# Seven products for eight: Strassen's scheme for the upper half of a gated block, with its sums on VectorE

## Chip, cores, metric

One core of a Trainium2 chip. The metric is the device time of one launch in microseconds (us), slowest core, median of several executions.

## The reference

```python
# attention: 4 batches, 8 heads, 768 positions, head size 64; a position attends to those
# whose six hash bits (signs of q @ proj) equal its own
mask = q_bucket[:, :, :, None] == k_bucket[:, :, None, :]
scores = np.where(mask, scale * np.matmul(q, k.transpose(0, 1, 3, 2)), -1e9)
attn = softmax(scores)                      # float32
x = (attn @ v)  ->  (3072 tokens, 512)
# gated block: w_gate, w_val (512, 1536), w_out (1536, 512)
g = x @ w_gate
silu = g * (1.0 / (1.0 + np.exp(-g)))
val = x @ w_val
return (silu * val @ w_out).astype(np.float32)
```

`x @ w_gate` and `x @ w_val` are the upper products, the product with `w_out` is the down product. The tokens of one batch are 768, in two halves of 384.

## The kernel before

The gated block of one batch is cut into 72 pieces ("atoms") that are woven into the attention of the next batch, in the order in which they are emitted. Each engine works off its own instructions in that order. After the last batch's attention, only the gated block is left.

```python
def norm(u):                                   # ends one half of a head pair
    ps = side_bank("sum")                      # a bank of its own
    for h in range(2):
        nc.tensor.matmul(ps[...], ones, t[:, h, :], start=True, stop=True)
    nc.vector.reciprocal(r, ps[:, 0:HQ])
    ...
    nc.vector.scalar_tensor_tensor(out=xT[b][:, pr, half * HQ : (half + 1) * HQ], ...)
    if pr == NP - 1 and half == 1:
        push_ffn(b)                            # x of the batch is complete: queue its atoms
...
def up(f, half, w, name):                      # 48 of these a batch: four fp32 matmuls each
    ps = bank(name)
    for j in range(NJ):
        nc.tensor.matmul(ps[:, 0:HQ], w[:, j, f * P : (f + 1) * P],
                         x[:, j, half * HQ : (half + 1) * HQ], start=j == 0, stop=j == NJ - 1)
    ...                                        # g: tanh on ScalarE, gate on VectorE; val: VectorE
def down(half, i, fs):                         # 24 of these a batch: three fp32 matmuls each
    for f in fs:
        nc.tensor.matmul(ps, hs[half][f][:, i * P : (i + 1) * P], wo[:, f, :], ...)
...
def hash_blocks():                             # hash of the next head pair
    ps = front_bank("hps")
    where = [(name, half) for name in "kq" for half in range(2)]
    for i, (name, half) in enumerate(where):
        nc.tensor.matmul(ps[i * BLOCK : (i + 1) * BLOCK, 0:HQ], hash_w[name][:, 0:BLOCK], ...)
    for i, (name, half) in enumerate(where):
        for to in (0, D):
            sign(name, half, ...)              # k: VectorE (kb), q: ScalarE (qb)
...
for u in range(0, N + 2, 2):                   # one iteration: two units of attention
    score(u); score(u + 1)                     # exp on ScalarE
    while due:
        norm(due.pop(0))
    for x in left:
        attend(x)                              # av on TensorE, acc on VectorE
    ...
    credit += rate                             # 3.1
    while atoms and credit >= 1.0:
        credit -= 1.0
        atoms.pop(0)()
        ...
```

The softmax here doesn't subtract the row's maximum and nothing guards it: scores larger than these inputs give would overflow.

## Time and profile before

| | before |
|---|---|
| time, median of 3 | 1139.44 us (1139.39 to 1139.5) |
| span of the profiled run | 1137.4 us |
| TensorE, VectorE, ScalarE busy | 1126.2, 538.4, 269.1 us |
| TensorE without work | 11.2 us (span less busy) |
| mean granted TensorE clock | 1.000 |

TensorE works 99% of the span. Of the 11 us without work, some 9 lie at the start and at the end, where the last output is written. Time can only be won where TensorE has less to do. The lines for this are in the prediction.

### The profile page before, as it was taken

What the parts mean: (1) busy time and instruction counts of PE and PEld (TensorE: products, weight loads), DVE (VectorE), ACT (ScalarE), POOL (GpSimd) and SP (SyncE); (2) the same over time, 40 slices, a digit from 0 to 9 for tenths busy, and PEclk for the clock granted to TensorE, in tenths of its full rate; (3) what the DMA queues carried; (4) which work ended last, traced back from release to release, by engine and by line L of the source; (5) the groups of instructions that cost most, each with busy time, mean ns of one, the idle gap of its engine ahead of it and who ended that gap; (6) DMA issues with size and microseconds to landing.
All of it is one profiled execution on the core that took longest, in us unless ns stands there. A gap on an engine that the chain in (4) does not pass through costs nothing.

```text
span 1137.4 us, 10768 instructions
## 1 busy us (share of the span) xinstructions
PE 1126.2 (99%) x4357; PEld 548.9 (48%) x4357; DVE 538.4 (47%) x783; ACT 269.1 (24%) x413; POOL 21.0 (2%) x57
## 2 busy tenths in 40 slices
PE   8999999999999999999999999999999999999998
PEld 3444445555444455555544445555544445555543
DVE  4899989899942244344442244444342222222100
ACT  4545221212212222122221223222131121010000
POOL 1000000000000000000000000000000000000000
PEclk9999999999999999999999999999999999999999
DMA  5333422423200220010002021010000000000000
GB/s 140 90 95 67 110 74 88 103 87 103 75 33 19 46 43 1 15 28 14 1 15 46 19 61 29 14 28 1 15 0 10 19 19 9 1 1 0 1 28 28
DMA packets 97842, 44.74 MB, mean 39 GB/s; under 512 B 86016, under 2 KB 90112, under 8 KB 97792
## 3 DMA queue, kind: packets, MB, share of 16 engines
q1 hardware_dynamic: 92032, 26.03, 10.0%
q0 software_dynamic: 4960, 17.83, 5.0%
q8 instruction: 34, 0.56, 0.2%
q10 hardware_dynamic: 800, 0.20, 0.1%
q14 instruction: 16, 0.13, 0.0%
HBM read 37.75 MB, written 6.29 MB: 39 GB/s over the span
## 4 chain that ended last, share of the span: by engine, by line
PE 96%; DVE 3%; ACT 0%; DMA 0%; issue 0%; SPq 0%; DVEq 0%; ACTq 0%
PE po L399 22%; PE g L378 22%; PE val L378 22%; PE sc L325 13%; PE av L336 11%; PE sum L357 2%; PE hps L276 2%; DVE acc L344 1%; PE tps L258 1%; PE hps L285 1%; DVE r L360 0%; DMA kraw<-in_k_dram 0%; PE idle L134 0%; DVE kb L271 0%; DVE wv L226 0%
## 5 line engine op out<-in xcount | busy, mean ns | idle before, releaser
L378 PE MATMUL val<-xT,wv 128*128 128x384 f32 x768 | 266.5, 490 | 0.3 <-DVE wv L226 0.3
L378 PE MATMUL g<-xT,wg 128*128 128x384 f32 x768 | 266.2, 490 | 0.0
L399 PE MATMUL po<-wo,ht 128*128 128x512 f32 x576 | 254.6, 597 | 0.0
L327 ACT ACTIVATE A<-sc 128x768 f32<-128x768 f32 x192 | 154.8, 812 | 192.6 <-PE sc L325 170.9
L378 PEld LDWEIGHTS val<-xT,wv 128*128 128x128 f32 x768 | 143.7, 190 | 111.5 <-issue 7.3
L378 PEld LDWEIGHTS g<-xT,wg 128*128 128x128 f32 x768 | 143.7, 190 | 110.8 <-DVE acc L344 6.0
L399 PEld LDWEIGHTS po<-wo,ht 128*128 128x128 f32 x576 | 107.4, 190 | 140.3 <-issue 138.9
L360 DVE RECIPROCAL r<-sum 128x384 f32<-128x384 f32 x32 | 81.8, 2556 | 176.1 <-PE sum L357 176.1
L325 PE MATMUL sc<-qT,kT 64*128 64x384 f32 x768 | 155.1, 482 | 0.0
L336 PE MATMUL av<-A,vraw 128*64 128x386 f32 x768 | 144.1, 496 | 0.0
L385 DVE SCALAR_TENSOR_TENSOR t<-t,g 128x384 f32<-128x384 f32 x96 | 53.0, 552 | 188.5 <-ACT t L384 188.5
L384 ACT ACTIVATE t<-g 128x384 f32<-128x384 f32 x96 | 47.1, 491 | 398.5 <-PE g L378 393.6
L344 DVE TENSOR_TENSOR acc<-acc,A 128x768 f32<-128x768 f32 x128 | 122.2, 955 | 34.0 <-ACT A L327 29.0
L390 DVE SCALAR_TENSOR_TENSOR ht<-t,val 128x384 f32<-128x384 f32 x96 | 52.9, 551 | 101.5 <-PE val L378 101.1
L336 PEld LDWEIGHTS av<-A,vraw 128*64 128x64 f32 x768 | 49.4, 136 | 81.3 <-issue 79.0
L325 PEld LDWEIGHTS sc<-qT,kT 64*128 64x128 f32 x768 | 68.7, 189 | 21.4 <-issue 21.4
L325 PE MATMUL sc<-qb,kb 64*128 64x384 bf16 x384 | 63.6, 328 | 0.8 <-DVE kb L271 0.8
L325 PEld LDWEIGHTS <-kb 64*128 64x128 bf16 x384 | 18.6, 93 | 68.7 <-issue 54.3
L403 ACT COPY o<-po 128x512 f32<-128x512 f32 x24 | 14.1, 586 | 155.6 <-PE po L399 155.3
L269 ACT ACTIVATE qb<-hps,columns 32x384 bf16<-32x384 f32 (+1 forms) x48 | 27.7, 577 | 77.3 <-DVE kb L271 44.6
L271 DVE TENSOR_SCALAR kb<-hps,columns 32x384 bf16<-32x384 f32 (+1 forms) x48 | 32.1, 669 | 24.2 <-PE hps L285 17.2
L340 DVE SCALAR_TENSOR_TENSOR acc<-A 128x768 f32<-128x768 f32 x32 | 30.4, 951 | 0.0
(69 smaller groups left out, 350.8 us busy)
## 6 DMA issues: line engine op xcount, KB each, us to landing
vraw<-in_v_dram SPq DMA_DIRECT2D x16, 384.0 KB, 3.1
words<-in_moe_w_val_dram POOLq DMA_DIRECT2D x12, 512.0 KB, 3.7
words<-in_moe_w_out_dram POOLq DMA_DIRECT2D x12, 512.0 KB, 3.5
out_dram<-o SPq DMA_DIRECT2D x24, 256.0 KB, 2.0
words<-in_moe_w_gate_dram POOLq DMA_DIRECT2D x10, 512.0 KB, 3.8
qraw<-in_q_dram SPq DMA_DIRECT2D x48, 96.0 KB, 3.1
kraw<-in_k_dram SPq DMA_DIRECT2D x46, 96.0 KB, 3.0
qraw<-in_q_dram SPq DMA_DIRECT2D x8, 192.0 KB, 3.5
```

The source lines that it names most:

```text
L271: nc.vector.tensor_scalar(o, ps[at, 0:HQ], scalar1=above_k[to], scalar2=times_k[to], op0=ALU.is_gt, op1=ALU.mult)
L325: nc.tensor.matmul(sc[:, h, 0:HQ], x["k", n][rows, ks], x["q", n][rows, qs], start=start, stop=not start)
L327: nc.scalar.activation(ring[u % RING][:, :, 0:HQ], sc[:, :, 0:HQ], AF.Exp, scale=SCALE)
L336: nc.tensor.matmul(ps[h * D : (h + 1) * D, 0:AW], raws["v", n][:, h, c, :], a[:, h, :], start=c == 0, stop=c == NCH - 1)
L340: nc.vector.scalar_tensor_tensor(out=acc[n, half], in0=ring[(u - 1) % RING][:, :, 0:HQ], scalar=S * EPS / P, in1=a[:, :, 0:HQ], op0=ALU.ad ...
L344: nc.vector.tensor_tensor(acc[n, half], acc[n, half], a[:, :, 0:HQ], op=ALU.add)
L360: nc.vector.reciprocal(r, ps[:, 0:HQ])
L378: nc.tensor.matmul(ps[:, 0:HQ], w[:, j, f * P : (f + 1) * P], x[:, j, half * HQ : (half + 1) * HQ], start=j == 0, stop=j == NJ - 1)
L384: nc.scalar.activation(t, ps[:, 0:HQ], AF.Tanh, scale=0.5)
L385: nc.vector.scalar_tensor_tensor(out=t, in0=t, scalar=1.0, in1=ps[:, 0:HQ], op0=ALU.add, op1=ALU.mult)
L390: nc.vector.scalar_tensor_tensor(out=ht, in0=now["t"], scalar=0.5, in1=ps[:, 0:HQ], op0=ALU.mult, op1=ALU.mult)
L399: nc.tensor.matmul(ps, hs[half][f][:, i * P : (i + 1) * P], wo[:, f, :], start=f == 0, stop=f == NF - 1)
```

## The change

Two 128-column blocks of a weight and the two token halves form a 2 by 2 block product over the two halves of the inner dimension 512. It takes eight block products, or seven by Strassen's scheme (in Winograd's form) with sums before and after. A block product is two fp32 matmuls of 128x384, half of what an `up` atom does. In each of batches two to four, twelve groups (six pairs of blocks, two weights) of seven products replace 48 atoms. The first batch keeps the plain products, as VectorE is still at work on the weights then.

Other parts of it: the bank kept for the norm's sums and the hash goes, these use score tiles (two, of two banks each), and the products get three banks for two. x is kept in one tile per head pair, some buffers shrink to make room, and the credit counts a product as 1 and every other atom as 2. Cut to its core:

```diff
-    aux_ps = ctx.enter_context(tc.tile_pool(name="aux_ps", bufs=1, space=PSUM))
-    mm_ps = ctx.enter_context(tc.tile_pool(name="mm_ps", bufs=2, space=PSUM))
+    mm_ps = ctx.enter_context(tc.tile_pool(name="mm_ps", bufs=3, space=PSUM))
...
-        ps = side_bank("sum")
+        ps = score_tile("sum")[:, 0, :] if atoms else bank("sum")
...
+    def up_strassen(x, hs, first):
+        lo, hi = halves
+        ...                                    # eight sums of x, emitted at once, on VectorE:
+            (t3[:, j], x[2 + j][:, hi], x[j][:, hi], subtract),
+            (t2[:, j], t3[:, j], x[j][:, lo], add),
+            (x[j][:, hi], x[j][:, hi], x[j][:, lo], subtract),
+            (t4[:, j], t2[:, j], x[2 + j][:, lo], subtract),
+        def combine(i):                        # sums of weights
+            if first:
+                nc.vector.tensor_tensor(s3, a11, s3, op=ALU.subtract)
+            nc.vector.tensor_tensor(s2, a22, s3, op=ALU.subtract)
+            nc.vector.tensor_tensor(s1, s2, a11, op=ALU.add)
+            nc.vector.tensor_tensor(s4, a12, s2, op=ALU.subtract)
+        ...
+            def step(n):                       # one atom: one product
+                if n == 0:
+                    combine(i + 1)
+                if n in (0, 1, 2, 6):
+                    now[n % 6 if n < 6 else 6] = bank("up")[:, 0:HQ]
+                if n == 0:
+                    product(b(0), a11, [x[j][:, lo] for j in range(2)], True)
+                    nc.scalar.copy(now["p1"], b(0))
+                elif n == 1:
+                    product(b(1), s2, [t2[:, j] for j in range(2)], True)
+                    add(now["u2"], now["p1"], b(1))
+                elif n == 2:
+                    product(b(2), s1, [x[j][:, hi] for j in range(2)], True)
+                    add(now["y"], now["p1"], b(2))
+                elif n == 3:
+                    product(b(0), a12, [x[2 + j][:, lo] for j in range(2)], False)
+                    done(0, 0, b(0), tile_of())   # gate: tanh on ScalarE, then VectorE
+                elif n == 4:
+                    product(b(1), s3, [t3[:, j] for j in range(2)], False)
+                    ...
+        combine(0)
+        for i in range(len(groups)):
+            group(i)
...
-        credit += rate
-        while atoms and credit >= 1.0:
+        credit += 6.2 if n < 2 * NP else 5.6
+        while atoms and credit >= atoms[0][0]:
```

## The prediction

> **What bounds the kernel now.** I read the page's busy shares first, then the slices, the chain and the groups, and last the timeline around the points where a batch of the gated block begins.
>
> ```profile
> PE 1126.2 (99%) x4357; PEld 548.9 (48%) x4357; DVE 538.4 (47%) x783; ACT 269.1 (24%) x413; POOL 21.0 (2%) x57
> PE   8999999999999999999999999999999999999998
> DVE  4899989899942244344442244444342222222100
> PEclk9999999999999999999999999999999999999999
> PE 96%; DVE 3%; ACT 0%; DMA 0%; issue 0%; SPq 0%; DVEq 0%; ACTq 0%
> L378 PE MATMUL val<-xT,wv 128*128 128x384 f32 x768 | 266.5, 490 | 0.3 <-DVE wv L226 0.3
> L378 PE MATMUL g<-xT,wg 128*128 128x384 f32 x768 | 266.2, 490 | 0.0
> L360 DVE RECIPROCAL r<-sum 128x384 f32<-128x384 f32 x32 | 81.8, 2556 | 176.1 <-PE sum L357 176.1
> L385 DVE SCALAR_TENSOR_TENSOR t<-t,g 128x384 f32<-128x384 f32 x96 | 53.0, 552 | 188.5 <-ACT t L384 188.5
> L344 DVE TENSOR_TENSOR acc<-acc,A 128x768 f32<-128x768 f32 x128 | 122.2, 955 | 34.0 <-ACT A L327 29.0
> ```
>
> TensorE is busy in every slice, at full clock, and 96% of the chain is its own. So time taken out of it counts in full as long as nothing makes it wait. The kernel calls 192 upper matmuls a batch; 1536 records for four batches means two records per fp32 call. The mean of 490 ns counts overlapped records twice, so I take the spacing from the last stage, where nothing else is interleaved. There a block of 8 records takes 2.58 us, 0.3225 us a record:
>
> ```profile
> 952.97 2.58 PE g L378 x8
> 955.55 2.58 PE val L378 x8
> ```
>
> The other thing to read is where a batch begins (here batch three, inside attention), and what the hash does to the queues:
>
> ```profile
> 673.94 0.34 PE L325 MATMUL sc<-qb,kb 64*128 64x384 bf16 x2
> ...
> 674.97 1.62 ACT L327 ACTIVATE A<-sc 128x768 f32<-128x768 f32 x2 [0.44 <-PE sc L325]
> 675.66 0.87 PE L357 MATMUL sum<-acc,ones 128*64 128x384 f32 x4
> 676.35 1.47 PE L336 MATMUL av<-A,vraw 128*64 128x386 f32 x8
> 676.57 2.56 DVE L360 RECIPROCAL r<-sum 128x384 f32<-128x384 f32 x1 [10.37 <-PE sum L357]
> 677.75 2.85 PE L378 MATMUL g<-xT,wg 128*128 128x384 f32 x8
> 679.19 0.62 DVE L363 SCALAR_TENSOR_TENSOR xT<-avs,e,r 128x384 f32<-128x384 f32 x1
> ...
> 761.47 2.72 DVE L271 TENSOR_SCALAR kb<-hps,columns 32x384 bf16<-32x384 f32 x4 [0.26 <-PE hps L285]
> 764.28 2.33 ACT L269 ACTIVATE qb<-hps,columns 32x384 bf16<-32x384 f32 x4 [6.97 <-DVE kb L271]
> 766.64 0.49 ACT L384 ACTIVATE t<-g 128x384 f32<-128x384 f32 x1
> ```
>
> TensorE starts the gated block at 677.75, although the last half of x is normed only at 679.8: the first blocks take the other half. Nothing waits today. The last three lines show the hash: VectorE reads its bank, then ScalarE, and the tanh behind it waits.
>
> **What the Trainium skill says.** (1) "TensorE: Matmul & The Clock Gate", Back-to-back issue gap: N/2.4 + 2.5 ns, 162.5 ns at N = 384. The trace's 322.5 ns a record is about twice that, as if each record passed its columns twice; I use the trace's number. (2) "VectorE: DVE Perf Modes", The TRN2 errata: an fp32 tensor_tensor takes (N+151)/0.96 ns. For 768 that is 957 ns, the trace has 955, so they agree. As estimates, 384 columns take 557 ns (the trace's 552 for a scalar_tensor_tensor from PSUM fits) and 256 take 424 ns. (3) "PSUM — Partial Sum Buffer", PSUM bank collisions: two engines must not be in the same bank and quadrant at once, reads included. The trace agrees: qb begins 0.09 us after kb ends. (4) The TensorE page again, What's actually happening: after an idle window of some 3.4 us the clock falls to half, until a busy window has passed. The kernel before has no such gap, and its clock line is flat.
>
> **The change, part by part.**
>
> *Removed.* Two blocks of outputs by two weights halves need 8 products before and 7 after. Per batch 192 calls become 168 (12 groups of 7 products of 2 calls): 48 records fewer, x 0.3225 = 15.5 us. Three batches: **46.4 us**, all on the path. A perfect result would be 1093.
>
> *Added on VectorE.* Per group: three weight sums of 256 (1.27 us) and six sums of 384 with a PSUM operand (3.34 us); the four gatings (2.21 us) were there. That is 6.82 us a group beside 14 x 0.645 = 9.03 us of TensorE. Per batch also eight sums of x (4.5 us), and in batch two a fourth weight sum a group (5.1 us in all). Sum: 12 x (1.27 + 3.34) + 4.5 = 59.8 us a batch, 185 us in all. VectorE goes to about 725 us, two thirds of the span. ScalarE gains 36 copies of 0.48, 17 us. On average both fit, so the question is bursts.
>
> *Steady work.* In the last stage I followed banks by hand: a product bank is wanted again two products (2.58 us) after its last matmul, and the two or three VectorE operations that free it (plus tanh of 0.49) take 1.0 to 1.4 us. It holds; no stall. In the interleaved iterations TensorE has 1.72 (scores) + 1.45 (av) + 5.6 products x 1.29 = 10.4 us; VectorE has 1.9 (acc) + 5.6 x 0.97 = 7.4, more with a norm (3.3), two transposes (1.9) or the hash (2.7).
>
> *Start of each changed batch.* This is the largest loss. The x sums need the half that the last norm writes, and the code queues on VectorE: reciprocal, xT (3.3 us together), eight x sums, then the weight sums, and only product one (t2, s2) can then go. Counted from the iteration's start: TensorE does scores, sums, av and product zero until 5.35 us. VectorE starts the reciprocal at 2.65 and has xT at 5.95. Operations without a wait between them follow each other some 0.08 us faster than their durations (in the trace the transpose starts 0.47 us after a 0.55 us gating), so eight sums at 0.48 and s2 end at 10.2, 10.6 with the extra sum of batch two. Stall: 5.25 and 4.85 us. In the last batch no av products lie in between: the norm's sums end, product zero takes 1.3 us, VectorE needs 2.6 + 0.7 + 3.8 + 0.4 = 7.6: stall 6.3. Together **16.4 us**.
>
> *Hash.* The hash now uses a score tile, and the copy of product zero queues on ScalarE behind qb, which waits for kb, which waits for VectorE's backlog. Following the queues by hand: in the second iteration of a batch, product three, which adds to the bank that this copy reads, waits about 2.75 us; one pair later the second score waits about 1 us for the hash's tile; one more pair later 0.2; in the down products about 0.7. That is some 4.7 us a batch, **9.5 us** for the two interleaved ones.
>
> *Norm sums.* They now take the score tile whose exp ends at 675.8 in the lines above, where the sums began at 675.66: 0.2 us each, 24 norms: **5 us** for the three interleaved stages.
>
> *Clock.* Three start stalls of 5 to 6 us are long enough to lose the clock; a window of 3.4 us at half speed costs 1.7 us, some 1 us on average each, as it isn't certain: **3 us**.
>
> Sum: 46.4 - 16.4 - 9.5 - 5 - 3 = 12.5 us gained. **1127 us**, 1.1% faster.
>
> **Rivals.**
>
> A: *the count of products alone*. Bursts are absorbed by the third bank and by the scores, where VectorE catches up. For it: VectorE stays at two thirds, and TensorE stands idle for 11 us at most today. Only a few starts would be lost: 1098 to 1108. Against it: the start's order of work is in the code, and VectorE runs in order.
>
> B: *VectorE becomes the bound inside attention*. An iteration with norm and transposes has 7.4 + 3.3 - 1.0 + 1.9 = 11.6 us of VectorE beside 10.4 to 11.1 of TensorE; gate groups add about 1 us of waiting on tanh. If every such iteration loses 2 us and every hash 3, another 10 to 15 us go and the time is 1138 to 1143. Against it: a pair of six iterations has about 56 us of VectorE in 66 of TensorE, and the remaining iterations pay it back.
>
> C: *each product of four records costs more than half a block of eight*, because more waits stand before a weight load; the first block after a switch takes 2.78 for 2.58. With 0.1 us on 252 products that would be 25 us, and the gain would be gone: about 1150. Against it: in the last stage blocks that each wait for a bank follow at an even 2.58.
>
> **Range and chances.** The saving is sure to a microsecond or two; the losses are an estimate of 34 us from following queues by hand, and could be 15 (rival A in part) or 50 (B in part). This gives 1104 to 1143. Over 2% faster means under 1116.7, losses below 24 us: 0.3. Slower by 2% needs losses of 69 us: 0.05. Within 2%: 0.65.
>
> **What would show it.** Upper product records should fall by 144, at an unchanged spacing (1.29 us a product). At each of the three batch starts TensorE should stand still for 5 to 6 us before a product, waiting on a VectorE weight sum or x sum, and the clock line may dip there. Sums should wait on the exp; a product or a score should wait near each hash. VectorE should show near 725 us busy. The prediction is wrong if those starts have no gap, if the spacing of products in the last stage is above 1.35 us, or if TensorE's idle time is spread over all interleaved products instead of these places.

## The result, and the profile after

1129.97 us (1128.81 to 1130.28, four runs) against 1139.47 of the kernel before in the same rounds. The ratio is 0.9914, interval 0.9897 to 0.9931. Ratios here are the mean time of one kernel's fast runs over that of the other's fast runs of the same rounds, so not quite the ratio of the medians quoted.

The parts of the page that answer to those shown of before (busy time, slices, chain):

```profile
PE 1093.0 (97%) x4213; PEld 525.5 (47%) x4213; DVE 700.7 (62%) x1143; ACT 284.8 (25%) x449; POOL 21.1 (2%) x57
...
PE   8999999999999989999999997999999997999998
...
DVE  4899989999932267777761337667674223667400
...
PEclk9999999999999989999999998999999998999999
...
PE 89%; DVE 6%; ACT 3%; issue 1%; DMA 0%; POOL 0%; SPq 0%; ACTq 0%; DVEq 0%; POOLq 0%
```

TensorE has 144 records fewer (4357 to 4213), as the count of products says. VectorE rose from 538 to 701 us. TensorE's line and its clock line now have dips in the same three slices, and VectorE and ScalarE have come into the chain. Who TensorE waited for, longest first (total us, times, longest), in the view of waits:

```profile
PE up L450 <- DVE ws L442: 15.8, 3, 6.0
PE up L450 <- ACT ht L483: 2.9, 1, 2.9
PE up L450 <- DVE c L378: 2.3, 1, 2.3
PE sum L359 <- ACT A L329: 2.2, 8, 1.0
...
PE sc L327 <- ACT qb L271: 0.9, 2, 0.6
```

Line 450 is the product, 442 the weight sum s2, 483 the copy of product zero, 378 the gate, 359 the norm's sums, 329 the exp, 271 the sign of q's hash. Three waits, one per changed batch, make up 15.8 us. Here is the last batch's, in the timeline (start, us, engine, line; the releaser in brackets):

```profile
944.84 0.87 PE L359 MATMUL sum<-acc,ones 128*64 128x384 f32 x4
...
945.64 1.56 PE L450 MATMUL up<-xT,wg 128*128 128x384 f32 x4
945.75 2.56 DVE L362 RECIPROCAL r<-sum 128x384 f32<-128x384 f32 x1 [14.85 <-PE sum L359]
...
948.37 0.62 DVE L365 SCALAR_TENSOR_TENSOR xT<-avs,e,r 128x384 f32<-128x384 f32 x1
948.91 1.02 DVE L423 TENSOR_TENSOR xc<-xT 128x384 f32<-128x384 f32 x2
...
951.72 1.02 DVE L423 TENSOR_TENSOR xc<-xc,xT 128x384 f32<-128x384 f32 x2
952.66 0.41 DVE L442 TENSOR_TENSOR ws<-wg 128x256 f32<-128x256 f32 x1
...
953.22 2.90 PE L450 MATMUL up<-xc,ws 128*128 128x384 f32 x4 [6.02 <-DVE ws L442]
...
955.91 2.05 PE L450 MATMUL up<-xT,ws 128*128 128x384 f32 x4
957.80 1.45 PE L450 MATMUL up<-xT,wg 128*128 128x384 f32 x4
```

Product zero goes at 945.64. VectorE then works without a pause through the reciprocal, xT, eight sums of x and one weight sum, and product one can go 6.02 us late. It is also slow: the next product starts 2.69 us after it, the one after 1.89 us later, and only then comes the usual 1.29 (957.80 to 959.09). The wait has cost the clock: the profile shows it at half from 950.28 to 957.10.

**Where the 46.4 us went**, by the trace. TensorE without work rose from 11.2 to 35.2 us: 24.0 lost. Of these 15.8 are the three starts (5.19, 4.63, 6.02), 6.2 lie beside a hash (2.31, 0.29, 2.94, 0.64), and the rest is mostly before norm sums. Work at half clock behind five of these waits lost some 11 us more: I took the start-to-start times of the products and scores behind each, less what they take elsewhere (2.9, 1.9, 2.2, 1.7, 2.0). The mean granted clock says 0.988, which would be 13.5 us, but it counts the idle time within the waits too. The half-clock stretches of the profile, cut to the time after each wait, give much the same as the spacing: 2.8, 1.7, 2.1, 1.7 and 1.9 us, 10.3 in all. 46.4 - 24.0 - 10.7 = 11.7, and the span fell by 9.2. Some 2.5 us are not assigned to a place.

### The profile page after: what moved, and what is told of

Same layout as the page of the kernel before. It is cut to its first block, busy times and chain, and to the rows that moved or that the text cites. A ratio compares the mean times of both kernels' runs of the same rounds, so it can differ in the third digit from the quotient of the medians.

```text
span 1128.2 us, 10837 instructions
## 1 busy us (share of the span) xinstructions
PE 1093.0 (97%) x4213; PEld 525.5 (47%) x4213; DVE 700.7 (62%) x1143; ACT 284.8 (25%) x449; POOL 21.1 (2%) x57
## 4 chain that ended last, share of the span: by engine, by line
PE 89%; DVE 6%; ACT 3%; issue 1%; DMA 0%; POOL 0%; SPq 0%; ACTq 0%; DVEq 0%; POOLq 0%
PE up L450 28%; PE po L526 22%; PE sc L327 12%; PE up L396 11%; PE av L338 11%; PE sum L359 2%; ACT A L329 2%; PE hps L278 2%; DVE r L362 1%; DVE kb L273 1%; ACT qb L271 1%; DVE xc L423 1%; DVE acc L346 1%; PE tps L260 1%; PE hps L287 0%
## 5 line engine op out<-in xcount | busy, mean ns | idle before, releaser
L450 PE MATMUL up<-xT,ws 128*128 128x384 f32 x288 | 108.7, 501 | 0.0
L450 PEld LDWEIGHTS up<-xT,ws 128*128 128x128 f32 x288 | 55.2, 195 | 44.6 <-issue 7.2
L462 DVE TENSOR_TENSOR ht<-ht,up 128x384 f32<-128x384 f32 x108 | 57.0, 548 | 25.9 <-PE up L450 23.3
L450 PE MATMUL up<-xc,ws 128*128 128x384 f32 x144 | 57.3, 523 | 15.8 <-DVE ws L442 15.8
L462 DVE TENSOR_TENSOR c<-c,up 128x384 f32<-128x384 f32 x108 | 57.6, 549 | 23.7 <-PE up L450 23.0
L396 PE MATMUL up<-xT,wg 128*128 128x384 f32 x192 | 66.9, 491 | 0.4 <-DVE kb L273 0.4
L396 PE MATMUL up<-xT,wv 128*128 128x384 f32 x192 | 66.9, 491 | 0.3 <-DVE wv L226 0.3
L377 ACT ACTIVATE c<-up 128x384 f32<-128x384 f32 x42 | 20.6, 491 | 184.0 <-PE up L396 100.9
L450 PE MATMUL up<-xT,wv 128*128 128x384 f32 x144 | 54.3, 501 | 2.9 <-ACT ht L483 2.9
L450 PE MATMUL up<-xc,wg 128*128 128x384 f32 x144 | 53.9, 498 | 2.3 <-DVE c L378 2.3
L450 PE MATMUL up<-xc,wv 128*128 128x384 f32 x144 | 53.2, 492 | 0.0
```

The lines of the kernel that those rows point to most:

```text
L377: nc.scalar.activation(th, g, AF.Tanh, scale=0.5)
L396: nc.tensor.matmul(ps, w[:, j, f * P : (f + 1) * P], x[j][:, halves[half]], start=j == 0, stop=j == NJ - 1)
L450: nc.tensor.matmul(ps, a[:, j], xs[j], start=start and j == 0, stop=j == 1, skip_group_check=True)
L462: nc.vector.tensor_tensor(out_, a, b, op=op)
```

## The experiments

My theory: the loss lies at a few places, where the order of work on VectorE and ScalarE makes TensorE wait, and the longer of those waits cost the clock as well. Rivals: VectorE is too busy inside attention, so that gaps would only move; short products cost more than their share; the slow products are a mark of the profile alone.

### The starts with TensorE kept occupied

```diff
+                if i == 0 and n == 1:
+                    for z in range(fill):      # 7, 6, 8 in batches two, three, four
+                        nc.tensor.matmul(now[1], ident, wo[:, z, 0:HQ], start=True, stop=True)
```

The result of these is overwritten by product one.

> The changed kernel with 7, 6 and 8 idle matmuls (their result is overwritten) put before product one of each batch, so that TensorE stays occupied in the wait of 5.2, 4.6 and 6.0 us but the wait itself stays. Theory (the waits also cost the clock, as the slow products after each show, some 2.9 us a wait): the three starts keep full clock and the time falls by about 8 us, to 1121 or 1122. Rival (the slow products are a mark of the profile, the waits alone cost): no change, 1129 to 1131.

1121.9 us (1121.55 to 1123.39), ratio 0.9851, clock 0.998. The first start, from the timeline:

```profile
403.85 4.68 PE L481 MATMUL up<-wo,ident 128*128 128x384 f32 x14
...
409.11 1.56 PE L450 MATMUL up<-xc,ws 128*128 128x384 f32 x4 [0.58 <-DVE ws L442]
```

Product one still starts where VectorE lets it, but the next one follows at 410.51, 1.40 us later, where it was 2.69. Idle work, with the time at which VectorE releases product one left as it was (in batch two 10.5 us after the iteration's first score, against 10.6), bought 8 us. So the clock is a cost of its own, and the rival of a mark in the profile falls. Not all of the 8 us belongs to the starts: the wait of 2.94 us at a hash, which was not touched, lost the clock in the changed kernel (1.7 us) and not here. The last section says why.

### The starts covered by work left over

```diff
-        credit += 6.2 if n < 2 * NP else 5.6
+        credit += 5.85 if n < 2 * NP else 5.35
```

> The changed kernel with 5.85 and 5.35 for 6.2 and 5.6 as the rate, so that two or so blocks of the down product are left when the next batch begins, and stand between its sums and its first product. No work is added. Theory (three starts of 15.8 us, plus some 8 us of lost clock): about 1106, and no gap of over 1.5 us at the starts. Rival (VectorE is too busy inside attention, so the wait moves to the next products): 1120 to 1130, with gaps later in the same batch.

1109.04 us, ratio 0.973, from three runs (1107.74 to 1109.05). A fourth, the profiled one, took 5830.66 us, over five times as long. Its matmul records are four to five times as long (a down-product record 2484 ns for 597). Its page has no clock line, so the 1.0 in its result is no measurement of the clock. I left it out and don't know its cause. So the kernel was profiled again:

> e4_cover again, because its profiled run took 5829 us and so its profile can't be read. Expected: 1107 to 1110 us, no gap of over 1.5 us at the three starts, the gaps near the hash still there.

1110.73 us in this one look. Its waits begin:

```profile
PE up L450 <- ACT ht L483: 2.9, 1, 2.9
PE sc L327 <- ACT qb L271: 2.9, 3, 1.5
PE up L450 <- DVE c L378: 2.3, 1, 2.3
```

The waits for the weight sum are gone, those beside the hash remain. The gain over the changed kernel is 20.9 us (1129.97 less 1109.04). I had expected 24: the 15.8 of the waits and some 8 of clock. The clock behind the three starts was 7.1 by the trace, and the lines show 2.0 given back: scores waited 2.9 us on the hash's sign of q instead of 0.9, as other products now stand beside the hash (this reason is not tested). 15.8 + 7.1 - 2.0 is 20.9, but so close a fit is luck: the one profile, of a single run, shows a span 19.3 us shorter, 13.2 of it idle time and 6.1 busy time of TensorE. So the gaps moved a little, but the rival of a busy VectorE expected 1120 to 1130.

### The hash of q in a tile of its own

```diff
-            ps = front_bank("hps")
+            banks = {name: front_bank("hps") for name in "kq"}
...
+                ps = banks[name]               # in both loops
```

Without this, the program makes ScalarE wait for VectorE before it reads the shared tile. In the changed kernel's timeline:

```profile
698.75 2.71 DVE L273 TENSOR_SCALAR kb<-hps,columns 32x384 bf16<-32x384 f32 x4
...
701.56 2.33 ACT L271 ACTIVATE qb<-hps,columns 32x384 bf16<-32x384 f32 x4 [3.32 <-PE up L450]
...
703.92 0.48 ACT L483 COPY ht<-up 128x384 f32<-128x384 f32 x1
...
704.45 2.90 PE L450 MATMUL up<-xT,wv 128*128 128x384 f32 x4 [2.94 <-ACT ht L483]
```

The hash's products ended at about 697.4. VectorE's backlog delays kb, kb delays qb, qb the copy of product zero, and product three, which adds to the copied bank, waits for that. (The bracket behind qb names a product that ended within 0.1 us of kb, at about 701.5; the instruction itself waits on kb's semaphore and on the hash's own product. In e5_hash the wait on kb's semaphore is gone from it.)

> The changed kernel with the hash of q in a score tile of its own, so that ScalarE needn't wait for VectorE's kb before qb. Theory (ScalarE held by qb delays the copy and the tanh that a bank waits for: gaps of 2.3, 0.3, 2.9 and 0.6 us, two of them with a loss of clock of 2.9): 10 to 12 us less, about 1118 to 1120. Rival (VectorE's own backlog holds these products, not ScalarE): under 4 us less.

1120.47 us (1120.33 to 1120.9), ratio 0.9835: 9.5 us less than the changed kernel, just under the 10 to 12 expected: the four waits are 6.2 us, and the clock behind two of them was 3.6 by the trace instead of twice 2.9. No wait beside a hash is left. What remains:

```profile
PE up L452 <- DVE ws L444: 15.8, 3, 6.0
PE sum L361 <- ACT A L331: 2.2, 8, 1.0
```

VectorE has as much to do as before, so it was ScalarE held by the program's wait, not VectorE's load.

### Both together

> Both: the rate of e4_cover and the second tile of e5_hash. Theory: the gains add, about 1093 to 1097, near the count of products alone (46.4 us under the kernel before, 1093). Rival (VectorE as the bound in attention): above 1110.

1096.52 us (1096.33 to 1097.06), ratio 0.9625, clock 1.000. TensorE has no wait on a weight sum, a gate or a copy of over 0.3 us:

```profile
PE 1081.1 (99%) x4213; PEld 521.9 (48%) x4213; DVE 701.2 (64%) x1143; ACT 284.1 (26%) x449; POOL 21.0 (2%) x57
```

```profile
PE sum L361 <- ACT A L331: 1.9, 9, 0.6
```

The gains add: 20.9 + 9.5 = 30.4, measured 33.5, and the time is within the 1093 to 1097 expected. Of the 3 us more, 2.0 are the waits of scores that the covered starts had moved to the hash. The kernel is 42.8 us faster than the one before in the same rounds, of the 46.4 that seven products for eight can give. It is the fastest of this study, and correct.

### How much room VectorE has

```diff
+            for _ in range(2):                 # on top of "both together"
                 nc.vector.tensor_tensor(s2, a22, s3, op=ALU.subtract)
                 nc.vector.tensor_tensor(s1, s2, a11, op=ALU.add)
                 nc.vector.tensor_tensor(s4, a12, s2, op=ALU.subtract)
```

> e6_best with the three weight sums of each group done twice (same values), 108 operations of 0.42 us, 45 us more of VectorE and nothing more for the others. Theory (VectorE has room in the averages and the gaps come from the order of work at a few places): less than 8 us slower than e6_best's 1096.5. Rival (VectorE close to the bound inside attention): 15 us or more slower.

1103.27 us, 6.8 us slower than e6_best. VectorE's busy time rose by 38.5 us (739.7 for 701.2), less than the 45 of the plain sum, since operations overlap a little. So a sixth of the added work reached the end. That is within what I expected, but close to the 8 I had drawn: VectorE isn't the bound, and its room isn't large. In the last stage val groups began to wait some 0.3 us each. Inside attention, gate products waited 2.5 us in three places, the longest 1.5 us (0.2 us in e6_best), so with this much more work the rival of a busy VectorE begins to come true there.

### No seven-product batch, and the last one alone

```diff
-        if b == 0:
+        if True:                               # e7_plain
+        if b < B - 1:                          # e8_tail
```

Both runs also keep the rate of 6.2 to the end, and in e8_tail the last batch makes the fourth weight sum of each group, as batch two does in the changed kernel.

> The changed kernel with the plain upper products in all four batches (rate 6.2 throughout): only the buffers, the score tiles for norm sums and hash, and the third product bank of the change remain. Step of the prediction on trial: norm sums in a score tile cost 0.2 us each, 5 us in all, and the hash something: 1142 to 1147. What the profile of the changed kernel suggests instead (1.4 us of idle time before sums): 1138 to 1142.

1142.11 us, ratio 1.0024 (1.0007 to 1.0041): the new buffers alone cost 2.7 us, 2.3 of which are fifteen waits of up to 0.16 us before norm sums. It lies between the two expectations, at the lower edge of the prediction's step (1142 to 1147) and 0.1 us above the second guess (1138 to 1142), so it doesn't decide between them.

> As e7_plain, but the last batch, which has no attention beside it, by the seven products. Theory: 15.5 us saved, less one start wait of 6.0 us and its clock of 2.9: 6 to 7 us faster than e7_plain. Rival (banks or the spacing of short products cost in the last stage too): under 3 us faster.

1135.8 us, 6.3 us faster than e7_plain. The one start wait was 6.48 us there, as this batch now has the extra weight sum; 15.5 - 6.5 leaves 9.0, and the clock takes most of the rest (0.997 granted). So in the last stage too the product of four records costs just its share.

## Why the prediction was right

- **The saving**, 46.4 us: right. 144 records fewer, products 1.29 us apart where nothing waits (957.80 to 959.09), and e6_best came within 3.6 us of it, 2.7 of which e7_plain puts down to the buffers.
- **Starts**, 16.4 us as 5.25, 4.85 and 6.3: measured 5.19, 4.63 and 6.02, with the releaser named. The order of emission, the durations of before and the spacing of 0.48 were enough. In e4_cover, with no work added or taken away, the three waits were gone.
- **Hash**, 9.5 us: measured 6.2 us of waits (two of 0.3 and 0.6, two of 2.3 and 2.9). That removing them gave 9.5 us in e5_hash is luck, as this has their lost clock in it and the prediction's 9.5 were waits alone. The chain was right, and in batch three so were the places: product three (2.94 for 2.75), one pair later a score (0.64 for 1). In batch two they weren't: I had assumed five products in its first iteration, but with the credit left over from the first batch there are nine, and the wait fell one pair later on a bank that a gate frees (2.31).
- **Reading of the hash's lines**: wrong in one point. I put the order of kb and qb down to the chip's rule on PSUM. But kb reads partitions 0 to 63 and qb 64 to 127, other quadrants, for which the Trainium skill, "PSUM — Partial Sum Buffer", PSUM bank collisions, asks no such order. It was the program's own wait, for the whole tile, and a second tile removed it: in e5_hash qb (694.73) even starts before kb (695.21).
- **VectorE's load**, 185 us more and 725 us busy: the page shows 700.7, as it counts overlapping operations once; summed one by one they rose by 182 us. The estimates of 424 ns (256 columns) and 557 ns (384 columns from PSUM) compare with 418 to 425 and 548 measured.
- **Norm sums**, 5 us for 24 norms: 2.2 us in the changed kernel, in eight places, one of 1.0 us and the rest under 0.25. In most places next to nothing was lost. By e7_plain 2.7 us for all that the buffers cost.
- **Clock**, 3 us: mis-sized, the largest error. It took 10.7 us, since it was lost behind five waits and not behind some of three, and one loss was 1.7 to 2.9 us instead of 1. Shorter waits for the norms and the hash (8.4 measured, 14.5 foreseen) made up for most of that. So the sum, 34 foreseen and 37 measured, was nearer than its terms, by luck. One sum of the range is wrong: losses of 15 us give 1108, not 1104, which would need 11.
- **Rivals**: A is what the kernel could have been; e6_best's 1096.5 is even under its 1098, but the changed kernel doesn't get there. B wasn't the cause, by e5_hash, e6_best and e9_double. C falls by e8_tail and by the spacing.

## What to carry to other kernels

When work is taken from the engine that bounds a kernel, ask first where the work that replaces it stands in line at the moment the next stage starts. A chain of eleven operations in one engine's queue hardly shows in a busy share, and was 5 us of standstill at each start here. Leaving a little of the last stage's work for that moment, and keeping reads by two engines out of one tile, gave 33 us here; the scheme as changed gave 9.5. A wait of TensorE of 2 us or more should be counted with the slow work that can follow it, here a third to four fifths of its own length where the clock was lost.

## What the Trainium skill lacked or had wrong

- "TensorE: Matmul & The Clock Gate", What's actually happening and HAM oscillation — how this bites in real kernels: the rule is to avoid idle gaps above some 3.4 us. Here gaps of 2.31 and 2.94 us were followed by half speed (the product behind took 2.62 and 2.84 us for some 1.3 to 1.4), while in e3_warm the gap of 2.94 us was not (its product of four records took 1.56 us). Gaps of 1.0 and, in e4_again, 1.5 us cost no clock. So the safe length is shorter than the rule's. What decided was not the length alone: within a trace, all stretches of half clock begin on one grid of 3.41 us (in the changed kernel at 407.56 and 28, 80, 87 and 159 steps later). At full clock, half clock followed where TensorE had been idle for 2.07 us or more of the 3.41 us before such an edge (2.31 in 499.72 to 503.13, 2.94 in 701.10 to 704.52), and not after 1.91 us (e8_tail, 950.72 to 954.13). In e3_warm an edge at 698.23 cut the gap of 2.94 us into 1.33 and 1.61 us. So the same gap of 2.94 us can cost the clock or not, by how it falls on the grid.
- The same page has no spacing for fp32 matmuls. Here a call is two records of 322.5 ns at 384 columns, each about twice its formula for one pass (162.5 ns). The skill counts the passes of fp32 on another page, but gives no time.
- "PSUM — Partial Sum Buffer", PSUM bank collisions: it asks for order by bank and quadrant. The program orders two engines' reads of one tile even in different quadrants (kb, then qb); two tiles took 9.5 us off. The page doesn't warn that guarding by the whole bank can have such a price.
- On a whole launch slowed as that of e4_cover was (5830.66 us for 1109, TensorE's records alone four to five times as long, no clock record) no page was found; the cause stays open.
